# Hashed attention and a soft mixture of experts on one core: how the first two pairs of heads are prepared

## Chip, cores and metric

One NeuronCore of a Trainium2 chip. The metric is the device time of one execution in microseconds; three timed executions were taken of the kernel before, and one more with the hardware profiler on.

## What is computed

Two stages. Attention over 32 heads (4 batches of 8), 768 positions, 64 dimensions, in which a query may look only at keys whose six hash bits equal its own; its output, laid out as 3072 tokens of 512 values, goes through a soft mixture of 8 experts.

```python
q_bits = (einsum('bhsd,dk->bhsk', q, proj) > 0)      # k_bits likewise; six bits make a bucket
mask   = q_bucket[..., :, None] == k_bucket[..., None, :]
scores = where(mask, (q @ k.T) / sqrt(64), -1e9)
attn   = softmax(scores) @ v                           # per head, 768 x 768
x      = attn as [3072, 512]
logits = x @ phi                                       # 32 slots
slot   = softmax over tokens(logits).T @ x             # then per expert relu(. @ w1) @ w2
out    = softmax over slots(logits) @ slot_out
```

## The kernel before

Heads are handled in pairs; the two heads of a pair lie on partitions 0 to 63 and 64 to 127 of one transfer. All work is emitted from one sorted list (`plan`): `STEADY` gives the due time of each step relative to its head (the unit is a sixth of a head), `ONCE` gives it for single steps, mostly those of the opening and the end. Each engine runs what it was given in that order, so the table is an order written by hand for PE (TensorE), ACT (ScalarE), DVE (VectorE), POOL (GpSimd) and the DMA queues of SP, ACT and POOL.

For each head there is an operand tile `XY` (three of them rotate), with two halves `Y` and `X`, each of 128 partitions by 2 sides (x=0 queries, x=1 keys) by 768. In `Y`, rows 0 to 63 hold the high part of the values, row 64 a row of shifts (queries) or ones (keys), rows 65 to 76 the hash bits as penalties, rows 96 to 127 low parts; `X` holds the rest of the split. Rows 64 to 95 are zeroed once, and row 64 of the key side set to one, by `first_y` and `first_rows` (L281 to L290).

Per head: `smax` (L407) multiplies rows 0 to 95 and DVE takes the maximum of each row over nine PSUM tiles (L421, L424); `shift` (L434) makes of the maxima a 128 by 12 table in `mz`; `shift_rows` (L446) turns it on PE (L449), ACT copies it to `mr` (L452), and a DMA puts it into row 64 of `XY`. Only then may `scores` (L456) of that head run: two matmuls into one PSUM tile (L465), then the exponential on ACT (L469). POOL adds the exponentials up (`acc`, L471) into one of three sum tiles `acc0` to `acc2`, and `av` (L484) multiplies them with the values on PE (L494). In the steady part PE interleaves the scores of one head with the maxima of the next.

Before a pair's heads can start: `load` (L203) fetches raw queries and keys of the pair into `raw`, two planes of the tile `stage`; `bits` (L360) multiplies them with the projections (L357) and compares (`over`, L351); `split_hi` (L308, ACT, line L311) rounds to the high part; `split_lo` (L313, POOL line L321 for the first two pairs) leaves the low part; `spread_y`, `spread_l`, `spread_x`, `spread_bits` (L328 to L403) move the pieces by DMA to the rows of `XY` (line L325).

The opening, for head 0, goes by special steps: `first_bits` (L374) multiplies, and ACT copies the 64 rows of head 0 straight into `Y`; `first_over` compares on DVE straight into `Y`; `first_last` copies the products of the bits to a spare tile, from which POOL makes the bits of both heads (`bits_rest`, L393), which the DMAs spread to head 1. `copy_ident` rounds the identity on POOL, `first_mz` zeroes `mz`. `keep_warm` (L254) and `spin` (L428) are matmuls whose results nobody reads; a spin follows each maximum of head 0. The second pair's raw values go into the same `raw` planes as the first's.

Of the kernel before, what the change touches and what calls it, by code (L numbers as in the profile page):

```python
# [90 lines left out]
    ('load_weights', 16): 147.216379, ('load_weights', 17): 153.5946, ('load_weights', 18): 156.8062,
    ('load_weights', 19): 165.5946, ('load_weights', 2): 39.9087, ('load_weights', 20): 168.8062,
    ('load_weights', 21): 177.5946, ('load_weights', 22): 189.5946, ('load_weights', 3): 51.9087,
    ('load_weights', 4): 63.9087, ('load_weights', 5): 83.361725, ('load_weights', 6): 87.216379,
    ('load_weights', 7): 95.361725, ('load_weights', 8): 99.216379, ('load_weights', 9): 107.361725,
# [7 lines left out]
    ('scores', 8, 0, 1): 49.396684, ('scores', 9, 2, 0): 55.21665, ('shift_rows', 0): -3.614750908,  # L103
# [46 lines left out]
def lsh_attention_soft_moe(  # L150
# [130 lines left out]
    def first_y(i):  # L281
        for ts in (Ys, Xs):
            nc.gpsimd.memset(ts[i][64:96].bitcast(F32), 0.0)
# [789 lines left out]
```

## Time and profile before

| what | us |
|---|---|
| median of three timed runs | 481.88 (481.84 to 482.64) |
| the profiled execution's own time | 480.13 |
| its span, from first to last instruction | 478.4 |
| PE busy | 461.8 |
| POOL busy, DVE busy, ACT busy | 330.5, 364.4, 250.3 |
| mean granted TensorE clock | 0.989 of full |

Times of rows count from the span's start. A timeline row gives start, length, engine, line, operation, the tiles it writes and reads, how many instructions it merges, and in brackets the idle time of the engine before it with what ended it. PE rows overlap, since matmuls are pipelined, so the distance of starts says more than the length.

### The profile page before, as it was taken

The numbers are of one execution on the slowest core, as the hardware profiler recorded it, in microseconds if no ns is written. First come the engines' busy times: TensorE is split into PE (matmuls) and PEld (weight loads), VectorE is DVE, ScalarE is ACT, GpSimd is POOL, SyncE is SP. The second block draws the span as 40 slices with busy tenths as digits, with TensorE's granted clock in tenths as the row PEclk, the third lists the DMA queues.
The fourth block names the chain that finished last, engine by engine and source line by source line (L and its number), as shares of the span: only waits on it lengthen the run. The fifth ranks groups of instructions, "written<-read, shape, count | busy, mean of one in ns | idle before, by whom it ended". The sixth has DMA issues, their size and how long they took to land.

```text
span 478.4 us, 10738 instructions
## 1 busy us (share of the span) xinstructions
PE 461.8 (97%) x4012; PEld 290.6 (61%) x4012; DVE 364.4 (76%) x690; ACT 250.3 (52%) x465; POOL 330.5 (69%) x236
## 2 busy tenths in 40 slices
PE   7799999999999999999999999999999999989992
PEld 4466666666666666666666565656656666453581
DVE  5658897979798888888888888888989766463242
ACT  4365555564666464555655564646655455431242
POOL 7868776969595969696868696968859696602200
PEclk9799999999999999999999999999999999999998
DMA  5668587868575757777767676767758388979967
GB/s 149 186 164 198 145 180 218 181 170 185 172 174 160 161 136 160 224 173 209 189 168 196 173 216 167 213 166 224 195 169 223 112 214 317 393 295 388 408 267 299
DMA packets 39697, 99.71 MB, mean 208 GB/s; under 512 B 7422, under 2 KB 13708, under 8 KB 39644
## 3 DMA queue, kind: packets, MB, share of 16 engines
q1 hardware_dynamic: 39260, 98.16, 71.6%
q0 software_dynamic: 224, 0.47, 0.5%
q8 instruction: 32, 0.52, 0.5%
q10 hardware_dynamic: 160, 0.39, 0.3%
q14 instruction: 21, 0.17, 0.1%
HBM read 52.76 MB, written 6.29 MB: 123 GB/s over the span
## 4 chain that ended last, share of the span: by engine, by line
PE 90%; DMA 2%; POOL 2%; DVE 2%; issue 1%; ACT 1%; SPq 1%; DVEq 0%; ACTq 0%; POOLq 0%
PE st L465 29%; PE av L494 27%; PE smx L418 15%; PE qh L904 3%; PE mi L556 3%; PE mi L506 2%; PE mi L521 2%; PE qs L986 2%; PE mi L357 2%; DMA out<-w 1%; PE mi L541 1%; PE mi L711 1%; PE qa L949 1%; POOL stage L321 1%; PE mi L449 1%
## 5 line engine op out<-in xcount | busy, mean ns | idle before, releaser
L482 POOL TENSOR_TENSOR acc<-acc,pt 128x768 f32<-128x768 f32 x125 | 229.2, 1834 | 9.1
L469 ACT ACTIVATE pt<-st 128x512 f32<-128x512 f32 x288 | 164.1, 596 | 49.0 <-PE st L465 41.0
L465 PE MATMUL st<-XY 128*128 128x512 f32 (+1 forms) x768 | 180.1, 346 | 0.0
L424 DVE TENSOR_REDUCE mx<-smx 128x1 f32<-128x512 f32 x192 | 130.6, 688 | 28.8 <-PE smx L418 25.3
L465 PEld LDWEIGHTS st<-XY 128*128 128x128 f32 x768 | 129.5, 190 | 16.3 <-issue 0.6
L494 PE MATMUL av<-pt,v 128*32 128x384 f32 x1536 | 136.2, 488 | 0.0
L418 PE MATMUL smx<-XY 96*128 96x256 f32 (+1 forms) x384 | 117.8, 360 | 1.6 <-DMA XY<-bt 0.7
L476 POOL TENSOR_TENSOR acc<-pt 128x768 f32<-128x768 f32 x32 | 58.7, 1835 | 65.8 <-ACT pt L469 65.8
L494 PEld LDWEIGHTS av<-pt,v 128*32 128x32 f32 x1536 | 46.4, 110 | 70.7 <-issue 70.5
L418 PEld LDWEIGHTS smx<-XY 96*128 96x128 f32 x384 | 68.7, 191 | 29.6 <-DVE mx L424 8.8
L421 DVE TENSOR_REDUCE mx<-smx 128x2 f32<-128x512 f32 x96 | 64.8, 675 | 4.3 <-PE smx L418 3.8
L498 ACT COPY avs<-av 128x384 f32<-128x384 f32 x32 | 15.3, 478 | 89.9 <-PE av L494 89.9
L318 DVE TENSOR_REDUCE stage<-stage 128x768 fp32r<-128x1536 f32 x28 | 50.1, 1790 | 0.0
L513 DVE RECIPROCAL sm<-sm 128x128 f32<-128x128 f32 x45 | 38.1, 896 | 0.0
L558 DVE TENSOR_TENSOR xq<-mi,r 128x256 f32<-128x256 f32 x45 | 17.6, 418 | 26.2 <-PE mi L556 26.2
L311 ACT ACTIVATE stage<-stage 128x768 fp32r<-128x768 f32 x30 | 24.9, 840 | 9.0 <-DMA stage<-qk 6.7
L556 PEld LDWEIGHTS mi<-ident,avs 128*128 128x128 f32 x90 | 10.2, 141 | 10.6 <-issue 10.0
L509 ACT ACTIVATE sm<-mi,eps 128x384 f32<-128x384 f32 x15 | 8.7, 582 | 13.8 <-PE mi L506 13.8
L943 POOL CAST avs<-lacc 128x48 fp32r<-128x48 f32 x8 | 2.1, 266 | 19.6 <-ACT lacc L934 12.5
L556 PE MATMUL mi<-ident,avs 128*128 128x128 f32 x90 | 15.7, 282 | 0.0
L986 PE MATMUL qs<-w 128*32 128x128 f32 (+1 forms) x360 | 15.5, 305 | 0.0
L904 PE MATMUL qh<-w,siT 128*32 128x512 f32 x128 | 14.6, 595 | 0.0
(179 smaller groups left out, 334.6 us busy)
## 6 DMA issues: line engine op xcount, KB each, us to landing
w<-w SPq DMA_DIRECT2D x61, 512.0 KB
XY<-stage SPq DMA_DIRECT2D x62, 384.0 KB
stage<-qk SPq DMA_DIRECT2D x32, 384.0 KB
XY<-stage SPq DMA_DIRECT2D x62, 192.0 KB
v<-vt SPq DMA_DIRECT2D x32, 192.0 KB
out<-w SPq DMA_DIRECT2D x12, 512.0 KB
xq<-w SPq DMA_DIRECT2D x3, 512.0 KB
XY<-bt SPq DMA_DIRECT2D x62, 19.5 KB
```

The source lines that it names most:

```text
L318: nc.vector.tensor_reduce(out=w[:, 2 * x + 1], in_=stage[:, x:n + 1:n - x].rearrange("p t s -> p s t"), axis=AX.X, op=ALU.add, negate=True)
L418: nc.tensor.matmul(pt[:, o:o + b - a], Ys[h % N_Y][0:96, 0, t * P:(t + 1) * P], Ys[h % N_Y][0:96, 1, a:b], start=True, stop=True)
L421: nc.vector.tensor_reduce(out=mx[:, n - 1:n + 1], in_=pt.rearrange("p (a x) -> p a x", a=2), axis=AX.X, op=ALU.max)
L424: nc.vector.reduce_max(out=mx[:, n:n + 1], in_=pt, axis=AX.X)
L465: nc.tensor.matmul(pt[:, o:o + b - a], x[:, 1, i * P:(i + 1) * P], x[:, 0, a:b], start=first, stop=not first)
L469: nc.scalar.activation(pts[i // 2][:, 512 * u:512 * u + 512], pt, AF.Exp, scale=D ** -0.5)
L476: nc.gpsimd.tensor_tensor(out=s["acc"], in0=pr[:, 0:S], in1=pr[:, S:2 * S], op=ALU.add)
L482: eng.tensor_tensor(out=s["acc"], in0=s["acc"], in1=pr[:, a * S:(a + 1) * S], op=ALU.add)
L494: nc.tensor.matmul(s["av"][D * c + d:D * c + d + 32, 0:HC], s["v"][:, i, d:d + 32], pr[:, o + c * HC:o + (c + 1) * HC], start=(i == 0), st ...
L513: nc.vector.reciprocal(out=rs[:, k * P:(k + 1) * P], in_=rs[:, k * P:(k + 1) * P])
L556: nc.tensor.transpose(pt[:, o:o + P], st[h + a]["avs"][:, k * P:(k + 1) * P], ident)
L904: nc.tensor.matmul(ph[fh][32 * j:32 * j + 32], siT[:, k, 4 * g + j, :], wt[0, g, k, j][:, fh * 512:(fh + 1) * 512], start=(k == 0), stop=( ...
```

## The change

The opening is laid out anew; nothing changes in `STEADY`. Raw values of the first pair come in halves of 64 partitions (head 0's keys, head 0's queries, then head 1's), behind the small transfer `first`; the remaining constants (`cst`) come later. The second pair's raw values go to the sum tiles `acc1` and `acc2`, which nobody uses yet, and are issued right behind. Zero rows and rows of ones are written by memsets in place, two of them on DVE, and no DMA carries them any more. `first_bits` multiplies only head 0's 64 rows, with 512 and 256 columns; a new step `more_bits` multiplies all 128 rows into one PSUM tile, which ACT copies for `bits_rest`. The comparisons for head 0 are five (one of 512, four of 256 columns). Twelve spins stand in the table at places of their own, reading the keys' side, and `keep_warm` is called for two matmuls at the start instead of seven, with the later lot of three gone.

```diff
-    def load(h, xs=(0, 1)):
-        for x in xs:
-            nc.sync.dma_start(out=raw[:, x], in_=qk[x, h // 2])
+    def raws(h, x):
+        return accs[1 + x] if h == 2 else raw[:, x]
+
+    def load(h):
+        for x in range(2):
+            nc.sync.dma_start(out=raws(h, x), in_=qk[x, h // 2])
+
+    def load_half(a):
+        for x in (1, 0):
+            nc.sync.dma_start(out=raw[D * a:D * a + D, x], in_=qk[x, 0, D * a:D * a + D])
...
-    load(0, (1,))
     nc.sync.dma_start(out=pre[:, 0:C_ID + 64], in_=first[:, 0:C_ID + 64])
-    load(0, (0,))
-    nc.sync.dma_start(out=pre[:, C_ID + 64:], in_=cst[:, C_ID:C_FD])
+    load_half(0)
+    load_half(1)
...
-    keep_warm(7, True)
+    keep_warm(2, True)
...
-    row = accs[0][0:1]
-    nc.gpsimd.memset(row, 1.0)
+    nc.vector.memset(Ys[0][64:96].bitcast(F32), 0.0)
+    nc.vector.memset(XYs[2][64:96, 0].bitcast(F32), 0.0)
...
-    def first_y(i):
-        for ts in (Ys, Xs):
-            nc.gpsimd.memset(ts[i][64:96].bitcast(F32), 0.0)
-
     def first_rows(i):
-        for ts in (Ys, Xs)[i == 0:]:
-            if i == 1:
-                move(ts[i][64:96], Xs[0][64:96], nc.gpsimd)
-            else:
-                nc.gpsimd.dma_start(out=ts[i][ROW:ROW + 1, 1].bitcast(F32), in_=row)
+        ts = XYs[i] if i else Xs[0]
+        nc.gpsimd.memset((ts[64:96, 1] if i == 2 else ts[64:96]).bitcast(F32), 0.0)
+        nc.gpsimd.memset(ts[ROW:ROW + 1, 1].bitcast(F32), 1.0)
...
+    def first_copy(x):
+        nc.scalar.copy(Ys[0][0:64, x], raw[0:64, x])
+
+    def first_bits(x):
+        first_pt[x] = p_st.tile([P, 512], F32, name="st")
+        for c, (a, b) in enumerate(((0, 512), (512, S))):
+            j = 2 * x + c
+            nc.tensor.matmul(first_pt[x][32 * j:32 * j + 32, 0:b - a], pb[0:D, 32 * x:32 * x + 32], raw[0:D, x, a:b],
+                             start=True, stop=True)
+
+    def first_hi(x):
         w = parts_of(0)
+        nc.scalar.copy(w[:, 2 * x], raw[:, x])
+
+    def more_bits():
+        pt = p_mi.tile([P, 512], F32, name="mi")
+        for x in range(2):
+            bits_of(0, x, pt)
...
+        nc.scalar.copy(pts[0][:, 0:HC], pt[:, 0:HC])
...
-        if h == 0 and n % 4 != 1:
-            spin(1)
```

ACT, from its first cast on: in the kernel before (L380, L382, L386 in `first_bits`, L390 and L391 in `first_last`, L349 `first_x`, L311 `split_hi` of the second pair, L452 the row of shifts, L325 the DMAs `spread_x` and `spread_l` of head 0).

```order
L380 CAST XY_134<-stage 64x768
L382 CAST stage<-stage 128x768
L380 CAST XY_134<-stage 64x768
L386 CAST stage<-stage 128x768
L390 COPY pt_82<-st 64x384
L391 COPY pt_82<-st 64x384
L349 COPY XY_134<-stage 64x768
L325 DMA XY_134<-stage 32x2x768
L349 COPY XY_134<-stage 64x768
L311 ACTIVATE stage<-stage 128x768 x2
L452 CAST mr<-mi 12x128
L325 DMA XY_134<-stage 32x2x768
```

And in the changed kernel (L391 `first_copy`, L402 `first_hi`, L409 the copy in `more_bits`, L327 `split_hi`, L365 `first_x`, L468 the row of shifts).

```order
L391 CAST XY_130<-stage 64x768
L402 CAST stage<-stage 128x768 x2
L409 COPY pt_82<-mi 128x384
L391 CAST XY_130<-stage 64x768
L327 ACTIVATE stage<-acc_86 128x768
L327 ACTIVATE stage<-acc_87 128x768
L341 DMA XY_130<-stage 32x2x768
L365 COPY XY_130<-stage 64x768
L341 DMA XY_130<-stage 32x2x768
L468 CAST mr<-mi 12x128
L365 COPY XY_130<-stage 64x768
```

The two `split_hi` of the second pair have moved from just ahead of the row of shifts to ahead of head 0's DMAs, and read the sum tiles; the copy of head 0's queries (the second L391) has moved behind the copy of the bits' products.

PE, from head 0's last maximum to its first scores, before (L418 `smax`, L432 `spin`, L449 the turn of `mz`, L357 the second pair's bits; `XY_134` is head 0, `XY_135` head 1).

```order
L418 MATMUL smx<-XY_134 128x256 x2
L432 MATMUL av<-XY_134 128x512
L449 MATMUL mi<-ident,mz 128x128
L357 MATMUL mi<-stage,pb 32x384 x4
L418 MATMUL smx<-XY_135 128x512 x2
L418 MATMUL smx<-XY_135 128x256 x2
L418 MATMUL smx<-XY_135 128x512 x2
L465 MATMUL st<-XY_134 128x512 x4
```

And in the changed kernel (L436 `smax`, L448 `spin`, L373 the bits, L465 the turn, L481 scores; `XY_130` is head 0, `XY_131` head 1).

```order
L436 MATMUL smx<-XY_130 128x512 x2
L448 MATMUL av<-XY_130 128x512 x2
L373 MATMUL mi<-acc_86,pb 32x384 x2
L373 MATMUL mi<-acc_87,pb 32x384 x2
L448 MATMUL av<-XY_130 128x512
L465 MATMUL mi<-ident,mz 128x128
L436 MATMUL smx<-XY_131 128x512
L436 MATMUL smx<-XY_131 128x256 x2
L448 MATMUL av<-XY_130 128x512
L436 MATMUL smx<-XY_131 128x512
L448 MATMUL av<-XY_130 128x512
L436 MATMUL smx<-XY_131 128x512 x2
L481 MATMUL st<-XY_130 128x512 x2
```

The bits of the second pair have moved from behind the turn to ahead of it, with three spins; ahead of the first scores stand five tiles of head 1's maxima in both (a pair of 256 columns is one tile), with two spins among them now.

POOL, from the first memset to the second pair's low parts, before (L283 `first_y`, L290 and L325 the DMAs of `first_rows`, L279 `ident`, L321 `split_lo`, L352 `bits_rest`).

```order
L276 MEMSET acc_85 1x768
L283 MEMSET XY_134 32x2x768 x2
L290 DMA XY_134<-acc_85 1x16x48
L325 DMA XY_135<-XY_134 32x2x768 x2
L279 CAST ident<-pt_83 128x128
L321 ISA
L321 TENSOR_TENSOR stage<-stage 128x768 x2
L273 MEMSET mz 128x128
L352 TENSOR_SCALAR bt<-pt_82,con 128x384
L283 MEMSET XY_136 32x2x768 x2
L290 DMA XY_136<-acc_85 1x16x48 x2
L321 TENSOR_TENSOR stage<-stage 128x768 x2
```

And in the changed kernel (L305 and L306 `first_rows`, L368 `bits_rest`, L337 `split_lo`, L295 `mz`, L301 `ident`).

```order
L305 MEMSET XY_131 32x3072
L306 MEMSET XY_131 1x1536
L368 ISA
L368 TENSOR_SCALAR bt<-pt_82,con 128x384
L337 TENSOR_TENSOR stage<-stage 128x768
L305 MEMSET XY_130 32x2x768
L306 MEMSET XY_130 1x768
L295 MEMSET mz 128x128
L301 CAST ident<-pt_83 128x128
L337 TENSOR_TENSOR stage<-stage 128x768
L305 MEMSET XY_132 32x1536
L306 MEMSET XY_132 1x1536
```

The DMAs are gone, `bits_rest` has moved from behind both low parts of the first pair to ahead of them, and head 0's zero rows stand between the two low parts; those of the second pair follow these rows in both.

## Rows read from the trace of the kernel before

**Rows 1.** The page: PE's busy time with its share of the span, and the granted TensorE clock in 40 slices of the span, in tenths of full.

```profile
PE 461.8 (97%) x4012; PEld 290.6 (61%) x4012; DVE 364.4 (76%) x690; ACT 250.3 (52%) x465; POOL 330.5 (69%) x236
...
PEclk9799999999999999999999999999999999999998
```

**Rows 2.** Windows of the opening and of the long middle: stretch in us, its length, busy us of each engine (instructions), granted clock, DMA share, GB/s.

```profile
0.00:4.00 4.00, 2.90 (x14) 2.30 (x14) 0.80 (x6) 1.73 (x3) 3.43 (x7) 1.00 0.51 150
4.00:10.82 6.82, 4.40 (x24) 2.29 (x23) 4.49 (x9) 3.83 (x6) 4.23 (x7) 1.00 0.56 142
10.82:14.23 3.41, 3.41 (x11) 2.49 (x9) 2.86 (x5) 1.58 (x2) 3.41 (x3) 0.50 0.91 233
14.23:21.06 6.83, 4.15 (x20) 1.85 (x18) 4.40 (x10) 1.83 (x3) 6.71 (x6) 1.00 0.58 162
21.06:24.47 3.41, 3.36 (x8) 2.34 (x8) 1.81 (x3) 0.98 (x2) 0.60 (x1) 0.50 0.67 160
...
40.00:475.03 435.03, 428.00 (x3829) 268.30 (x3821) 339.20 (x641) 229.14 (x430) 299.84 (x209) 1.00 0.74 213
```

**Rows 3.** The chain of work that ended last, its part in the opening: start us, us, what.

```profile
4.50 2.55 DMA XY<-acc
...
8.85 3.59 POOL stage L321 x2
...
12.58 1.66 POOL bt L352
...
16.84 1.93 DMA XY<-bt
...
26.16 0.23 PE smx L418
```

**Rows 4.** SP's DMA issues in the opening.

```profile
0.74 0.40 SPq L205 DMA_DIRECT2D stage<-qk  x1
1.20 0.42 SPq L223 DMA_DIRECT2D pt<-first  x1
...
10.68 2.11 SPq L205 DMA_DIRECT2D stage<-qk  x2
...
18.43 0.77 SPq L325 DMA_DIRECT2D XY<-mr  x1
```

**Rows 5.** ACT in the opening.

```profile
6.21 0.83 ACT L380 CAST XY<-stage 64x768 fp32r<-64x768 f32 x1 [0.89 <-DMA stage<-qk]
...
7.80 0.47 ACT L390 COPY pt<-st 64x384 f32<-64x384 f32 x1
...
17.42 0.84 ACT L311 ACTIVATE stage<-stage 128x768 fp32r<-128x768 f32 x1 [1.74 <-DMA stage<-qk]
...
18.17 0.24 ACT L452 CAST mr<-mi 12x128 fp32r<-12x128 f32 x1
```

**Rows 6.** DVE in the opening.

```profile
1.12 0.48 DVE L227 MEMSET phs<- 128x512 f32 x1
3.94 0.23 DVE L235 TENSOR_TENSOR pb<-pt 128x64 f32<-128x64 f32 x1 [2.33 <-DMA pt<-first]
...
5.18 1.38 DVE L352 TENSOR_SCALAR XY<-st,con 16x384 fp32r<-16x384 f32 x2 [0.94 <-PE st L357]
...
8.44 0.69 DVE L424 TENSOR_REDUCE mx<-smx 128x1 f32<-128x512 f32 x1 [0.65 <-PE smx L418]
...
13.12 0.69 DVE L424 TENSOR_REDUCE mx<-smx 128x1 f32<-128x512 f32 x1 [0.17 <-PE smx L418]
13.98 1.35 DVE L424 TENSOR_REDUCE mx<-smx 128x1 f32<-128x512 f32 x2 [0.16 <-PE smx L418]
15.26 0.69 DVE L421 TENSOR_REDUCE mx<-smx 128x2 f32<-128x512 f32 x1
...
16.48 0.17 DVE L442 SCALAR_TENSOR_TENSOR mz<-mi,mz 128x6 f32<-128x6 f32 x1
```

**Rows 7.** PE in the opening.

```profile
6.23 0.84 PE L357 MATMUL st<-stage,pb 128*32 128x384 f32 x4 [1.17 <-DMA stage<-qk]
...
7.93 0.47 PE L418 MATMUL smx<-XY 96*128 96x512 f32 x1 [0.22 <-DVE XY L352]
...
15.06 0.42 PE L432 MATMUL av<-XY 96*128 96x512 f32 x1
16.79 0.30 PE L449 MATMUL mi<-ident,mz 128*128 128x128 f32 x1 [1.31 <-DVE mz L442]
17.02 1.26 PE L357 MATMUL mi<-stage,pb 128*32 128x384 f32 x8
...
22.14 1.91 PE L465 MATMUL st<-XY 128*128 128x512 f32 x4
...
29.33 4.08 PE L494 MATMUL av<-pt,v 128*32 128x384 f32 x48
```

**Rows 8.** POOL in the opening.

```profile
0.74 0.73 POOL L276 MEMSET acc<- 1x768 f32 x1 [0.29 <-POOLq L1064]
1.50 2.69 POOL L283 MEMSET XY<- 32x1536 f32 x2
...
8.51 0.29 POOL L279 CAST ident<-pt 128x128 fp32r<-128x128 f32 x1
...
27.34 1.83 POOL L476 TENSOR_TENSOR acc<-pt 128x768 f32<-128x768 f32 x1 [5.68 <-ACT pt L469]
```

More of the change, by code (lines that the diff above doesn't have):

```diff
@@ L91 @@
[L91 to L95, printed above, removed]
+    ('batch_top_exp',): 195.7222, ('batch_turn', 3): 195.723, ('bits', 2): -23.689255146,
@@ L115 @@
+    ('spread_y', 27): 150.008401, ('spread_y', 29): 162.008401, ('spread_y', 3): 6.008401,
+    ('spread_y', 31): 174.008401,
 }
@@ L320, in split_lo @@
         else:
-            nc.gpsimd.tensor_tensor(out=w[:, 2 * x + 1], in0=raw[:, x], in1=w[:, 2 * x], op=ALU.subtract)
+            nc.gpsimd.tensor_tensor(out=w[:, 2 * x + 1], in0=raws(h, x), in1=w[:, 2 * x], op=ALU.subtract)
     def move(dst, src, eng=nc.sync):
@@ L349, in first_x, with over @@
         nc.scalar.copy(Xs[0][0:64, x], st[0]["w4"][0:64, 3 * x])
-    def over(out, pt, rows, eng=nc.vector):
-        eng.tensor_scalar(out=out, in0=pt[rows, 0:HC], scalar1=con[rows, C_TH:C_TH + 1],
+    def over(out, pt, rows, eng=nc.vector, cols=slice(0, HC)):
+        eng.tensor_scalar(out=out, in0=pt[rows, cols], scalar1=con[rows, C_TH:C_TH + 1],
                           scalar2=con[rows, C_AM:C_AM + 1], op0=ALU.is_gt, op1=ALU.mult)
@@ L357, in bits_of @@
             nc.tensor.matmul(pt[32 * j:32 * j + 32, 0:HC], pb[:, 32 * x:32 * x + 32],
-                             raw[:, x, (j % 2) * HC:(j % 2 + 1) * HC], start=True, stop=True)
+                             raws(h, x)[:, (j % 2) * HC:(j % 2 + 1) * HC], start=True, stop=True)
     def bits(h):
@@ L368, in lsh_attention_soft_moe, with first_over @@
     first_pt = {}
[L370 to L391 removed]
+    def first_over(x, a, b):
+        j = 2 * x + a // 512
+        over(Ys[0][64:80, x, a:b], first_pt[x], slice(32 * j, 32 * j + 16), cols=slice(a % 512, a % 512 + b - a))
+    def first_copy(x):
[7 more added lines that the diff above has]
+    def first_hi(x):
+        w = parts_of(0)
+        nc.scalar.copy(w[:, 2 * x], raw[:, x])
[3 more added lines that the diff above has]
+            bits_of(0, x, pt)
+        st[0]["bt"] = st[1]["bt"] = pp.tile([P, HC], F32R, name="bt", bufs=1)
+        nc.scalar.copy(pts[0][:, 0:HC], pt[:, 0:HC])
     def bits_rest():
@@ L776, in at @@
         plan.append((when, len(plan), (f, *args)))
-    first_y(0)
-    first_rows(0)
-    for i in range(1, N_Y):
-        if i > 1:
-            at(first_y, i)
+    for i in range(N_Y):
         at(first_rows, i)
@@ L785, in lsh_attention_soft_moe @@
     at(load_phi)
-    at(keep_warm, 3, True, tag="a")
+    at(load_cst)
     at(copy_ident)
-    at(first_bits)
-    at(first_last)
+    for n in (1, 0):
+        at(first_copy, n)
+        at(first_bits, n)
+        at(first_hi, n)
+    for xab in ((1, 0, 512), (0, 0, 256), (1, 512, S), (0, 256, 512), (0, 512, S)):
+        at(first_over, *xab)
+    at(more_bits)
+    for n in range(12):
+        at(spin, 1, tag=n)
     at(bits_rest)
```

82 lines of the change are left out of this document (40 added, 42 removed).

## The prediction

> **What bounds the kernel now.** First the page [rows 1]: TensorE (PE) is busy 461.8 us, 97% of the span; the only slices in which its granted clock is below full are in the first 25 us and at the end. Then the windows [rows 2]: from 40 to 475 us PE is busy 428.0 of 435.0 us at clock 1.00, so there time is PE work, and nothing in this change alters that work. A change of the opening can help only by letting PE reach its unbroken stretch sooner. In the PE rows [rows 7] that stretch starts with the first scores (L465) at 22.14 us; I take as the finishing line the first attend block (L494) at 29.33 us, because the change leaves PE's list behind it as it was. A shift of this block should reach the end nearly whole: what follows (weights, output) is issued as PE frees buffers, so it moves with it.
>
> What made PE wait until 22.14 us? The chain [rows 3] goes back through GpSimd (POOL): the zero rows and the row of ones for the first head, whose DMA takes 2.55 us; the two low parts, 3.59 us; the bits of the pair, 1.66 us; the DMA of those bits, 1.93 us; then the second head's maxima. Beside it runs a second chain that ends within a step of it: first head's maxima on VectorE (DVE), from 8.44 to 15.95 us [rows 6]; the shift (three small operations, to 16.64 us); its turn on PE at 16.79 us [rows 7]; and the copy of the result on ScalarE (ACT), which begins only at 18.17 us [rows 5], since ACT stands until 17.42 us for the second pair's raw values and then works 0.84 us on them. Those were issued only from 10.68 us on, as they go into the buffer that the first pair leaves [rows 4]. The row of shifts is sent at 18.43 us [rows 4].
>
> The clock is the third thing [rows 2]: 1.2 GHz (0.50) in 10.82 to 14.23 us, behind a stretch in which PE was busy 4.40 of 6.82 us, and again in 21.06 to 24.47 us, behind one with 4.15 of 6.83 us. The second low stretch lies on the first scores.
>
> **The change, part by part.** *Second pair at once, into the sums' buffers.* ACT's copy of the shift row no longer stands behind raw values: they are issued at about 3.1 and 3.5 us. The first sum buffer used so is written late (the first sum of all, in another buffer, is at 27.34 us [rows 8]), so the buffers are free. Gain: up to 18.17 - 17.09 = 1.1 us on the second chain. Issue of each transfer stays at 0.4 us [rows 4].
>
> *Zero rows in place.* POOL loses the 0.73 us memset, two memsets of 1.35 us each from its early list, the wait for its own DMA and two DMA issues, 8.51 us in all before `ident` [rows 8]. It gains one memset of 2.7 us and one of 1.4 us (two times 0.73), ended near 4.9 us, before the values for the bits exist. The bits then start when ACT has copied them (8.0 us below) and are done at 9.7, against 14.24; one low part follows to 11.5, and the rest of the list (2.1 us of memsets, `mz`, `ident`) ends about 14.0, before the shift at 16 us and the turn. So the first chain becomes some 4 us shorter and drops out. DVE takes over two memsets of 1536 elements: 512 took 0.48 us [rows 6], so 1.3 to 1.45 us each, on DVE from about 3.3 us to 6.1 us, in front of the first comparisons. Five of these (one of 512, four of 256 columns; two of 384 took 1.38 us [rows 6]) end at about 8.7 us. They are covered by the step below, with 0.5 us to spare.
>
> *Halves.* In before, the bits of x=0 started at 6.23 us when their 384 KB landed [rows 7]. The new queue has the same bytes ahead of the last half (without one 64 KB piece), in four transfers for two. I take 6.2 us for the last half; it can't well land before 5.3 (the last issue at 2.6 us, and 2.7 from the issue of the small `first` to its use [rows 4, 6]). No row shows raw values fetched by halves. The Trainium skill (DMA: Bandwidth & Descriptors, Rules for kernel authors) speaks against this edit: two transfers to disjoint halves of the partitions share the same engines and serialize, so one transfer is as good. By that rule the last half lands as the whole did, at 6.2 us, and the sum stays as below; with a last half at 5.3 us it would be 0.9 us less. An earlier first half is worth nothing here for a reason in the order: the first maxima need `first_copy` of x=0, and this now stands last on ACT, behind the bits of both halves.
>
> So: last half 6.2, eight bit matmuls 1.26 [rows 7] to 7.5, their copy 0.47 [rows 5] to 8.0, `first_copy` 0.83 [rows 5] to 8.8, matmul to maximum 0.51 (7.93 to 8.44 us [rows 6, 7]): **first maximum at 9.3 us**, 0.9 us later than before. But then nine follow without a gap: 0.65 us apart at full clock (13.98, two in 1.35 [rows 6]), I take 0.68: the seventh ends at 14.1, the ninth at 15.4, the shift is ready at 16.1.
>
> *The turn.* PE's list has, between the ninth maximum's matmul and the turn, two spins, the bits of the second pair and one more spin. At 0.06 + 0.24 for the matmul, 0.45 a spin (15.06 us row, 0.42 [rows 7]) and 1.26 for the bits this is 14.1 + 0.3 + 0.9 + 1.26 + 0.45 = **17.0 us**, later than the shift: the bits were behind the turn in before and are ahead of it now, price up to 0.9 us. Turn 0.30, cast 0.24 [rows 5, 7]: sent at 17.65 us, against 18.43.
>
> *The row's trip.* Bounds: 1.93 us from issue to landing of the last bits, and 3.71 us from the row's issue (18.43) to the first scores (22.14), in which other work also lay [rows 3, 4, 7]. I take 2.7, near the 2.55 of the other single-row DMA [rows 3]. First scores 20.35 us. The second head's maxima don't delay that: both orders put five of its nine tiles ahead of the first scores; from 17.2 us at 0.65 the third ends near 19.5 and the fifth matmul near 20.0. The edit named last in the change is thus worth nothing by itself.
>
> *Clock.* PE drops five of its first seven fp32 matmuls and all three of the second lot, and gets twelve spins for nine. Ahead of 4 us PE had worked 2.90 us [rows 2]; now about 0.9 us there and the bits from 3.6 on. So I allow for 1.2 GHz on the first bits (1.26 us become 2.5 if all run so, of which 0.5 is met if the last half lands at 5.7) and for one low stretch somewhere before the scores. At 0.86 us a tile for 0.65 (from 13.12 to 13.98 us, [rows 6]), four tiles cost 0.8; over the bits it costs 1.3; in front of the maxima next to nothing: I add 0.5. First scores: **20.9 us**, 1.2 us sooner.
>
> *From there to the attend block.* 12 matmuls of 512 columns and 12 of 256 for the scores, 4 and 6 for maxima, at 0.235 and 0.12 (0.23 for one of 512 [rows 3]), and a turn of 0.11: 3.76 + 2.16 + 0.11 = 6.0 us at full clock. Before took 29.33 - 22.14 = 7.2, of which 2.3 us fell in the low stretch. With a full clock, as PE is busier ahead of 21 us: 1.2 us more. Attend block at 26.9: **2.4 us gained**. The profiled execution took 480.13 us (span 478.4), so 477.7 for it; the median of the three timed runs is 481.88, 1.75 us above it, and the same step from there gives **479.5 us**.
>
> **Rivals.** (1) *The clock falls on the first scores again.* PE still waits for the row until 20.9 us, and in before such a stretch brought 0.50. The Trainium skill (TensorE: Matmul & The Clock Gate, HAM oscillation) has the same warning: gaps throttle the array again; both low stretches of this trace agree with it. Against it: spins now lie between the second head's maxima. Price 1.2 to 1.7 us: 480.9.
> (2) *Only the wait changes its name.* Last half late, first maximum at 10, a low clock on maxima and bits: first scores at 22, clock as before: no change, 481.9.
> (3) *Slower.* The bits in front of the turn are the place: at 1.2 GHz spins and bits take 2.6 us more, the turn comes at 19.6 and the first scores at 23.0; with the low stretch on the scores too (7.7 us to the attend block, as all 3.4 us of it then count) the block is at 30.7, 1.4 us late: 483.3. It decides at a turn later than 18.3 us. For it: the list has eight warming matmuls fewer at the start.
> (4) *More:* half landed at 5.3, no low stretch after 8 us, row's trip 2.0: scores at 19.0, attend block at 25.0: 477.6.
>
> **How the numbers follow.** About 0.2% (1 us) is what a measurement can tell from no change. Forecast 0.50 (own range 478.7 to 480.4), rival 1 0.20 (480.2 to 481.5), rival 2 0.12, rival 3 0.09, rival 4 0.09. Faster than 480.9: forecast, rival 4 and half of rival 1, 0.70; within: the other half and nearly all of rival 2, 0.21; slower 0.09. The range leaves out rival 3 and the far half of 4 and of 2: 478.0 to 481.8.
>
> **What would show it.** Right: first maximum near 9.3 us and nine without gaps; the turn near 17, its cast at once; first scores near 21 at clock 1.00; the attend block at 26 to 27.5; the same spacing of all that follows. Wrong: the turn waiting on PE's bits past 18 us; a low stretch on the scores; POOL's low part or memsets named as releaser of the shift or of the second head's rows; or the lead lost between 30 us and the end.

## Result and profile after

The changed kernel takes 484.09 us (median of 7 runs, 482.71 to 486.25) against 481.84 us (480.64 to 482.64) for the kernel before on the same chip: ratio 1.0053, 95% interval 1.0035 to 1.0071, 2.3 us slower. Forecast was 2.4 us faster. The profiled execution took 482.71 us. Its page, to be held against [rows 1]:

```profile
span 480.9 us, 10726 instructions
...
PE 466.0 (97%) x4007; PEld 289.8 (60%) x4007; DVE 367.6 (76%) x693; ACT 249.8 (52%) x464; POOL 330.8 (69%) x232
...
PEclk9999999999999999999999999999999999999998
```

PE is busy 4.2 us longer, with five instructions fewer: nearly the same matmuls, at a lower clock and, as the rows below show, with spins that wait for each other. The clock row hides it, and so does the clock column of the windows (length, then busy us of PE, PEld, DVE, ACT, POOL with counts, granted clock, DMA share, GB/s):

```profile
7.00:14.35 7.35, 6.90 (x20) 3.21 (x20) 4.92 (x9) 3.83 (x7) 4.47 (x3) 1.00 0.55 162
14.35:23.45 9.10, 8.79 (x25) 4.44 (x25) 5.46 (x12) 1.51 (x3) 8.79 (x9) 1.00 0.49 112
23.45:31.20 7.75, 7.56 (x41) 5.97 (x40) 6.90 (x14) 4.87 (x10) 2.83 (x3) 1.00 0.59 165
...
42.00:477.00 435.00, 428.34 (x3829) 268.31 (x3821) 338.98 (x640) 228.86 (x430) 299.97 (x209) 1.00 0.74 213
```

1.00 is printed wherever no record of the clock precedes, and the first record of this execution is a rise at 23.45 us. (So it is in the first window of [rows 2] too: the first record there is the rise at 4.0 us.) What PE had before that is read from its rows: start, length, line, operation, count, idle time before.

```profile
7.59 1.50 PE L373 MATMUL mi<-stage,pb 128*32 128x384 f32 x8 [0.34 <-DMA stage<-qk]
9.02 1.65 PE L448 MATMUL av<-XY 96*128 96x512 f32 x2
10.47 1.17 PE L436 MATMUL smx<-XY 96*128 96x512 f32 x3
11.44 1.48 PE L448 MATMUL av<-XY 96*128 96x512 f32 x2
12.72 1.05 PE L436 MATMUL smx<-XY 96*128 96x512 f32 x2
13.57 0.63 PE L448 MATMUL av<-XY 96*128 96x512 f32 x1
...
18.44 1.48 PE L448 MATMUL av<-XY 96*128 96x512 f32 x2
19.85 1.51 PE L373 MATMUL mi<-acc,pb 128*32 128x384 f32 x8
21.29 0.80 PE L448 MATMUL av<-XY 96*128 96x512 f32 x1
21.88 0.42 PE L465 MATMUL mi<-ident,mz 128*128 128x128 f32 x1
...
25.12 0.63 PE L481 MATMUL st<-XY 128*128 128x512 f32 x2
25.59 0.40 PE L436 MATMUL smx<-XY 96*128 96x256 f32 x2
...
31.20 3.11 PE L510 MATMUL av<-pt,v 128*32 128x384 f32 x36
```

From 12.72 us two maxima take 0.85 us, up to the start of the spin at 13.57: 0.43 for each 512 columns. From 25.12 us two matmuls of 512 columns take 0.47. So PE ran at 1.2 GHz over bits, all first maxima and the turn, and at 2.4 GHz from 23.45 us: no low stretch lies on the scores, unlike [rows 2]. In a pair of spins the second starts 0.69 to 0.85 us behind the first (9.02 and 9.88, 11.44 and 12.12 us): each spin takes the one buffer of its pool anew and waits until the spin before it has ended, so PE also waits within its own list. The rest of the chain to the turn and beyond, rows of DVE, ACT, POOL and SP against [rows 4 to 6] and [rows 8]:

```profile
11.25 0.69 DVE L442 TENSOR_REDUCE mx<-smx 128x1 f32<-128x512 f32 x1 [1.52 <-PE smx L436]
...
18.25 1.29 DVE L442 TENSOR_REDUCE mx<-smx 128x1 f32<-128x512 f32 x2 [1.01 <-PE smx L436]
...
20.06 0.17 DVE L458 SCALAR_TENSOR_TENSOR mz<-mi,mz 128x6 f32<-128x6 f32 x1
...
22.33 0.26 ACT L468 CAST mr<-mi 12x128 fp32r<-12x128 f32 x1 [7.46 <-PE mi L465]
...
15.71 0.29 POOL L301 CAST ident<-pt 128x128 fp32r<-128x128 f32 x1
...
22.65 0.83 SPq L341 DMA_DIRECT2D XY<-mr  x1
```

The shift is ready at 20.23 us, the turn comes at 21.88, behind spins and bits; ACT, which had been waiting 7.46 us, copies at once; POOL's part of the turn was done by 16.0 us. Against before the attend block is 1.86 us late, the third head's outputs 3.5 and all later heads 2.9, the end 2.6 (480.94 and 478.35 us). The extra us comes at 47 us, in the chain of waits:

```profile
40.15 1.43 SPq L341
41.62 6.30 DMA XY<-stage
47.92 0.14 issue
48.06 0.94 PE st L481 x3
```

The third head's `spread_x` stands in SP's list behind the fourth head's pieces and lands when PE wants to begin its scores.

### The profile page after: what moved, and what is told of

The parts are those of the page before. It is cut to its first block, busy times and chain, and to the rows that moved or that the text cites. A ratio compares the mean times of both kernels' runs of the same rounds, so it can differ in the third digit from the quotient of the medians.

```text
span 480.9 us, 10726 instructions
## 1 busy us (share of the span) xinstructions
PE 466.0 (97%) x4007; PEld 289.8 (60%) x4007; DVE 367.6 (76%) x693; ACT 249.8 (52%) x464; POOL 330.8 (69%) x232
## 4 chain that ended last, share of the span: by engine, by line
PE 89%; DMA 4%; SPq 2%; DVE 2%; ACT 1%; issue 1%; POOL 0%; DVEq 0%; ACTq 0%
PE st L481 27%; PE av L510 25%; PE smx L436 15%; PE qh L923 3%; PE mi L572 3%; PE mi L522 2%; PE mi L373 2%; PE mi L537 2%; PE qs L1005 2%; SPq L341 2%; DMA out<-w 1%; PE av L448 1%; DMA XY<-stage 1%; PE mi L557 1%; DMA stage<-qk 1%; PE mi L727 1%
## 5 line engine op out<-in xcount | busy, mean ns | idle before, releaser
L481 PE MATMUL st<-XY 128*128 128x512 f32 (+1 forms) x768 | 179.8, 345 | 0.6 <-DMA XY<-stage 0.3
L481 PEld LDWEIGHTS st<-XY 128*128 128x128 f32 x768 | 129.0, 190 | 17.2 <-issue 0.6
L436 PE MATMUL smx<-XY 96*128 96x256 f32 (+1 forms) x384 | 118.7, 364 | 0.4 <-DVE mx L439 0.2
L436 PEld LDWEIGHTS smx<-XY 96*128 96x128 f32 x384 | 69.4, 194 | 28.6 <-DVE mx L442 9.2
L327 ACT ACTIVATE stage<-stage 128x768 fp32r<-128x768 f32 x28 | 23.1, 840 | 9.5 <-DMA stage<-qk 6.3
L572 PEld LDWEIGHTS mi<-ident,avs 128*128 128x128 f32 x90 | 10.2, 141 | 10.6 <-issue 10.0
```

The source lines that it names most:

```text
L436: nc.tensor.matmul(pt[:, o:o + b - a], Ys[h % N_Y][0:96, 0, t * P:(t + 1) * P], Ys[h % N_Y][0:96, 1, a:b], start=True, stop=True)
L481: nc.tensor.matmul(pt[:, o:o + b - a], x[:, 1, i * P:(i + 1) * P], x[:, 0, a:b], start=first, stop=not first)
L572: nc.tensor.transpose(pt[:, o:o + P], st[h + a]["avs"][:, k * P:(k + 1) * P], ident)
```

## Experiments

Medians against the kernel before beside each (ratio with its 95% interval); "low" is what the profile shows of 1.2 GHz ahead of the attend block. "From the start", or "to" a time, means that the first record is the rise at that time; in the other rows the first record is a rise at 3.9 to 6.6 us, and what lies ahead of it is left out. Marks are of the profiled execution, us; its own time is in the last column, and where it lies 1.3 us or more off the median (before, after, e3, e5, e7, f13, f16) the marks need not be those of the median execution.

| run | median | ratio | low | turn | first scores | block | own |
|---|---|---|---|---|---|---|---|
| before | 481.84 | 1 | 10.82–14.23, 21.06–24.47 | 16.79 | 22.14 | 29.33 | 480.13 |
| after | 484.09 | 1.0053 (1.0035–1.0071) | from the start to 23.45 | 21.88 | 25.12 | 31.20 | 482.71 |
| e1 | 483.67 | 1.0027 (1.0007–1.0048) | to 27.37 | 21.64 | 25.45 | 32.55 | 484.38 |
| e2 | 483.89 | 1.0046 (1.0029–1.0063) | to 23.71 | 22.10 | 25.35 | 31.43 | 483.73 |
| e3 | 484.58 | 1.0057 (1.0036–1.0077) | to 23.34 | 20.31 | 25.30 | 31.36 | 482.54 |
| e4 | 485.89 | 1.0087 (1.0066–1.0108) | to 27.55 | 21.49 | 25.29 | 32.38 | 485.96 |
| e5 | 483.72 | 1.0037 (1.0016–1.0058) | 11.75–21.99 | 20.59 | 23.83 | 29.88 | 480.96 |
| e7 | 484.34 | 1.0045 (1.0028–1.0063) | 13.39–27.05 | 20.0 | 25.53 | 32.34 | 485.75 |
| e6 | 483.22 | 1.0027 (1.0009–1.0044) | to 16.83, 23.66–27.07 | 18.79 | 22.98 | 30.66 | 483.15 |
| e8 | 484.24 | 1.0055 (1.0036–1.0074) | 11.81–25.47 | 16.79 | 25.38 | 31.57 | 483.92 |
| e9 | 480.51 | 0.9962 (0.9948–0.9976) | to 14.35, 21.18–24.59 | 18.40 | 21.80 | 29.12 | 480.51 |
| e10 | 482.89 | 1.0008 (0.9988–1.0029) | 8.67–15.49, 18.91–25.73 | 18.12 | 23.05 | 30.35 | 482.44 |
| e11 | 484.04 | 1.0060 (1.0034–1.0086) | 16.26–29.91 | 16.30 | 24.58 | 33.13 | 484.17 |
| e12 | 481.40 | 0.9987 (0.9973–1.0001) | 9.87–16.70, 23.53–26.94 | 18.54 | 22.65 | 30.33 | 481.57 |
| f13 | 483.92 | 1.0036 (1.0022–1.0050) | to 16.80, 20.22–27.04 | 19.11 | 23.81 | 31.36 | 482.49 |
| f14 | 480.55 | 0.9972 (0.9961–0.9982) | 7.46–14.29, 21.12–24.53 | 18.42 | 21.79 | 29.11 | 481.01 |
| f15 | 480.86 | 0.9987 (0.9974–0.9999) | to 16.48 | 19.39 | 22.50 | 28.57 | 480.14 |
| f16 | 482.60 | 1.0017 (0.9998–1.0036) | 10.75–27.82 | 16.68 | 22.69 | 31.16 | 486.43 |
| f17 | 480.78 | 0.9994 (0.9977–1.0010) | to 15.18, 22.00–25.42 | 18.70 | 21.81 | 29.65 | 480.80 |
| f18 | 481.48 | 0.9993 (0.9975–1.0010) | to 22.00 | 20.02 | 23.52 | 30.04 | 482.10 |

### One part undone in the changed kernel

**e1**, warming:
```diff
-    keep_warm(2, True)
+    keep_warm(7, True)
```


> Changed kernel with seven warming matmuls at the start again instead of two. Theory 'clock': the changed kernel runs PE at 1.2 GHz from the start to 23.45 us, because two matmuls do not lift it; with seven it is lifted near 4 us, first scores come before 22.5 us (25.1 now), the attend block before 28.5 (31.2), the time is 481.0 or less (484.1 now). Rival 'raw values': the late last half (7.6 us) and ACT's order hold the chain; attend block at 30.5 or later, time 483.4 or more.

Three of its twelve times are 480.96 to 481.39, the other nine 483.26 to 485.27. The profiled one, of the nine, kept 1.2 GHz to 27.37 us, and its mean granted clock is 0.995, since the stretch without a record counts as full; the three have 0.986, as e5's profile below has with its early rise. So warming lifts the clock early in some executions; in the median it is not the main cause.

**e2**, two whole transfers:
```diff
-    load_half(0)
-    load_half(1)
+    for x in (1, 0):
+        nc.sync.dma_start(out=raw[:, x], in_=qk[x, 0])
```


> Changed kernel with the first pair's raw values in two whole transfers (keys first) instead of four halves. Theory 'halves': a transfer to 64 partitions runs at about half the rate, so whole ones land the last raw value near 6.2 us instead of 7.6, and the first maximum comes about 1.3 us sooner; time 482.8 to 483.3. Theory 'clock' alone: PE stays at 1.2 GHz and paces the maxima, less than 0.5 us comes out at the end, 483.6 or more.

No difference. The first maximum came at 11.47 us, 0.2 later than with halves: the whole pair was there sooner, but PE at 1.2 GHz worked on its bits without a wait to 7.81 us.

**e3**, the second pair's bits behind the turn:
```diff
-    ... ('bits', 2): -23.689255146,
+    ... ('bits', 2): -20.02,
```


> Changed kernel with the second pair's bits behind the turn of the first head's shifts, as in the kernel before. Theory 'bits ahead of the turn': the turn comes when the shift is ready, 20.3 us instead of 21.9, and the first scores 1 to 1.6 us sooner, 482.5 to 483.1. Rival: the second head's maxima, which then wait for the comparison of these bits on DVE, hold the first scores just as long; within 0.4 us of the changed kernel, 483.7 to 484.4.

The turn is 1.57 us earlier and the first scores are where they were: the bits then stand ahead of the second head's maxima, for which the scores wait as well. So the edit that I had named for rival 3 was not it. The wait at 47 us was gone, and the time no better.

**e4**, the third head's `spread_x` earlier:
```diff
-    ... ('spread_x', 2): 9.510813397,
+    ... ('spread_x', 2): 6.0,
```


> Changed kernel with the queries' side of head 2 (spread_x of head 2) issued on SP ahead of head 3's pieces instead of behind them. Theory 'queue': head 2's scores wait 1 us for these pieces in the changed kernel; issued early they don't, the heads from the third on are 1.9 us late against the kernel before instead of 2.9, time 483.0 to 483.3. Rival: contention of the transfers, whatever their order; 483.8 or more.

Worse: the piece now stands ahead of the fourth head's bits on SP, and PE waits 1.6 us for those (DMA `XY<-bt`) instead.

**e5**, `keep_warm(15, True)`, and **e7**, the same with e2's and e3's edits:

> Changed kernel with fifteen warming matmuls at the start, without a gap until the first bits. Theory 'clock': the run with seven fell into two groups of times (three of twelve near 481.1, the others 483.3 to 485.3), so seven lift the clock only sometimes; fifteen lift it before 8 us in nearly every execution. The first bits then start near 7 us instead of 4.5 but at 2.4 GHz, the first maximum comes by 11.5, the turn by 19, the attend block by 28.5; median 480.5 to 481.5. Rival: the raw values and ACT's order set the opening; two groups or one near 484 stay, median 483 or more.

> Changed kernel with fifteen warming matmuls, whole transfers of the first pair's raw values, and the second pair's bits behind the turn. If the parts add up: turn by 17.5 us, first scores by 21, attend block by 27, median 479.5 to 480.5, below the kernel before. If the maxima of the second head behind the bits set the first scores: as with fifteen warming matmuls alone, 480.5 to 481.5.

In both a rise near 5 to 6.6 us is lost again at 11.75 and 13.39 us, over the first maxima, and does not come back before 21.99 and 27.05 us. Warming at the start sets where the clock begins, and does not keep it there; e5's profile is the fastest of its twelve executions, 2.8 us under their median.

### The kernel before, with one part changed

**e6**, `keep_warm(2, True)` and none of the later three:

> Kernel before with two warming matmuls at the start instead of seven, and without the later three: only this part of the change. Theory 'clock': PE stays at 1.2 GHz through the first head's maxima or longer, median 1 to 2.5 us above the kernel before. Rival: POOL's chain and not PE set the first scores in the kernel before, so the clock up to 20 us costs it nothing; within 0.5 us of the kernel before.

1.3 us slower. Cold as the changed kernel is, it rises at 16.83 us, among the first maxima. Its list there differs from the changed one in the spins, among other things.

**e8**, a spin behind each of the second head's five tiles too:
```diff
-        if h == 0 and n % 4 != 1:
+        if h == 0 and n % 4 != 1 or h == 1 and n in (0, 2, 3, 8, 11):
```


> Kernel before with one more spin behind each of the five second-head maxima that stand ahead of the first scores. Theory 'clock': PE has fewer gaps from 19 to 22 us, the low stretch on the first scores (21.06 to 24.47 us) falls away more often, median 0.5 to 1.2 us below the kernel before. Rival: gaps at 18.3 to 19.0 us remain and the clock falls as before; within 0.4 us.

Slower, for a reason of its own: spins of this kernel read the queries' side, whose row of shifts is on its way.

```profile
21.41 0.77 PE L432 MATMUL av<-XY 96*128 96x512 f32 x1 [1.61 <-DMA XY<-mr]
```

**e11**, the second pair into the sums' buffers at once, alone:
```diff
-    ... ('load', 2): -12.762070462,
+    ... ('load', 2): -60.0,
...
+    def raws(h, x):
+        return accs[1 + x] if h == 2 else raw[:, x]
```


> The kernel before with one part of the change alone: the second pair's raw values go to the sums' buffers at once. Theory: the copy on ScalarE no longer stands behind them, the row of shifts is sent 0.7 to 1.1 us earlier (17.4 to 17.8 us for 18.43), but GpSimd's chain (zero rows, low parts, bits, their DMA) ends where it did and holds the second head's maxima, so first scores move by less than 0.6 us and the median lies within 0.5 us of the kernel before. Rival, the row alone decides: scores and block 1 us earlier, median 481.0.

Neither theory: 2.2 us slower. POOL's and SP's rows:

```profile
4.50 0.66 POOL L293 DMA_DIRECT2D XY<-acc  x1 [0.31 <-POOL XY L286]
9.15 1.12 POOL L328 DMA_DIRECT2D XY<-XY  x2 [3.99 <-DMA XY<-acc]
...
14.42 1.65 POOL L355 TENSOR_SCALAR bt<-pt,con 128x384 fp32r<-128x384 f32 x1
...
16.09 3.29 SPq L328 DMA_DIRECT2D XY<-bt  x4
19.43 0.72 SPq L328 DMA_DIRECT2D XY<-stage  x1
20.26 0.77 SPq L328 DMA_DIRECT2D XY<-mr  x1
```

With 768 KB more in flight POOL's one-row DMA took 4.4 us for 2.6 [rows 3], everything behind it on POOL came 1.84 us later, and the row of shifts, copied at 17.33 us, stood on SP behind four issues of bits to 20.26. So in this kernel the edit costs time as long as the rows go through POOL's queue.

**e12**, those rows written in place by POOL and the bits ahead of the second low part, on top of e11:
```diff
+        if i == 1:
+            nc.gpsimd.memset(XYs[1][64:96].bitcast(F32), 0.0)
+        ts = XYs[i] if i else Xs[0]
+        nc.gpsimd.memset(ts[ROW:ROW + 1, 1].bitcast(F32), 1.0)
...
-    ... ('bits_rest',): -37.319143276, ...
+    ... ('bits_rest',): -50.0, ...
-    ... ('first_last',): -38.392596163, ...
+    ... ('first_last',): -50.5, ...
```


> The kernel before with two parts of the change: the sums' buffers as above, and the zero rows and rows of ones written in place by GpSimd memsets with no DMA; the bits of both heads on GpSimd ahead of the second low part. Whole transfers, seven warming matmuls and the spins behind each maximum stay. Theory, both chains were needed: row sent near 17.5 us, first scores near 20.3 for 22.1, block near 27.5 to 28 for 29.3, median 480 to 481, faster than both kernels. Rival, the clock falls on the scores whenever they come after a wait: scores earlier, but the block within 0.7 us of before, median 481.5 to 482.3.

2.6 us faster than e11, level with before. The row was sent no earlier (19.15 us): a copy of 128 by 3 values on DVE, 0.16 us long in the kernel before, took 2.56 us, and the first comparisons began at 7.00 us for 5.18 [rows 6]. DVE's rows, and POOL's beside them:

```profile
4.29 2.56 DVE L240 COPY con<-pt 128x3 f32<-128x3 f32 x1
7.00 2.78 DVE L352 TENSOR_SCALAR XY<-st,con 16x384 fp32r<-16x384 f32 x4 [0.15 <-PE st L357]
...
4.17 2.65 POOL L288 MEMSET XY<- 32x3072 f32 x1
```

The copy ends at 6.85 us, with POOL's memset (6.82). In the changed kernel the same copy took 0.72 us, from 2.70 to 3.42, and the same memset there ended at 3.39.

**f16**, no spins behind the first maxima:
```diff
-        if h == 0 and n % 4 != 1:
-            spin(1)
```


> The kernel before without the nine spins behind the first head's maxima (matmuls that nobody reads), nothing else. Theory, the spins without a gap bring the clock back: after its fall at about 10.8 us it does not rise before the second head's maxima or the scores, turn at 17.5 us or later, block at 31 us or later (29.3), median 483.5 to 485. Rival, the spins are idle ballast: the same or 0.3 us faster.

In the theory's direction, and smaller: +0.7 us, with an interval that takes in 1, and times from 481.04 to 486.43. The profiled execution, the longest, shows what the theory said, 0.50 over all 17 us. What the shorter ones had is not shown: their mean granted clock, 0.976 to 0.989 for 0.978 here, does not set them apart.

```profile
10.75:27.82 17.07, 14.85 (x39) 8.45 (x40) 10.44 (x19) 5.79 (x9) 10.74 (x9) 0.50 0.67 184
```

### The spins put back in the changed kernel

**e9**, a spin behind each of the first head's nine tiles, as before, and none in the table:
```diff
             nc.vector.reduce_max(out=mx[:, n:n + 1], in_=pt, axis=AX.X)
+        if h == 0 and n % 4 != 1:
+            spin(1)
...
-    for n in range(12):
-        at(spin, 1, tag=n)
```


> The changed kernel with its twelve spins taken from their places in the table and put back behind each of head 0's nine maxima, as the kernel before has them; nothing else differs (two warming matmuls, halves, bits ahead of the turn). Theory, the spins' places: at 1.2 GHz a tile of maxima with its spin keeps PE without a gap, so the clock comes up within the first maxima (about 15 to 17 us in place of 23.4), the turn at 20 us or before (21.9), first scores at 23 or before (25.1), attend block by 29.5 (31.2); median 482.0 to 482.8. Rival, the start of the clock alone (fewer warming matmuls): the clock stays at 1.2 GHz until the second head's maxima as in the changed kernel, turn past 21, block past 31, median 483.5 or more.

By the medians 3.6 us faster than the changed kernel (4.4 by the two ratios), 1.3 faster than the kernel before. PE's rows, and the windows up to and on the scores:

```profile
10.06 0.80 PE L436 MATMUL smx<-XY 96*128 96x512 f32 x1 [1.33 <-ACT XY L391]
10.66 0.63 PE L450 MATMUL av<-XY 96*128 96x512 f32 x1
11.08 0.63 PE L436 MATMUL smx<-XY 96*128 96x256 f32 x2
...
13.22 0.63 PE L450 MATMUL av<-XY 96*128 96x512 f32 x1
13.64 0.63 PE L436 MATMUL smx<-XY 96*128 96x256 f32 x2
14.07 0.53 PE L450 MATMUL av<-XY 96*128 96x512 f32 x1
14.44 0.40 PE L436 MATMUL smx<-XY 96*128 96x256 f32 x2
...
17.00 0.85 PE L373 MATMUL mi<-acc,pb 128*32 128x384 f32 x8
18.40 0.30 PE L467 MATMUL mi<-ident,mz 128*128 128x128 f32 x1 [0.54 <-DVE mz L460]
```

```profile
14.35:21.18 6.83, 5.47 (x24) 2.63 (x23) 6.41 (x13) 1.20 (x3) 6.52 (x8) 1.00 0.69 153
21.18:24.59 3.41, 3.39 (x9) 2.81 (x10) 1.95 (x3) 1.02 (x2) 2.81 (x2) 0.50 0.70 240
```

From 11.08 us maxima and spins start 0.43 us apart, and the wait of a spin for the one before it is covered by the maxima between them; at 14.35 us the clock rises, and the bits take 0.85 us for 1.51. The turn waits 0.54 us for the shift, not for PE's list. The edit does two things at once: spins no longer stand in pairs among the maxima, and one spin instead of three stands between the last maximum and the turn.

**e10**, e9 with e1's and e3's edits; **f13**, e9 with e3's; **f14**, e9 with e1's; **f15**, e9 with e2's:

> The same, with seven warming matmuls at the start for two and the second pair's bits on PE behind the turn. Theory: the clock is lost at most for one stretch, as in the kernel before; turn at 18 to 19 us (shift ready decides, no bits ahead), first scores at 21 to 22, block at 28 to 29; median 481 to 482, no slower than the kernel before. Rival (halves and the second pair's transfers make the first bits so late that nothing is left, or the bits only move the clock's loss to the scores): block past 30, median 483 or more.

> The version with spins back (480.51 us), with one more edit: the second pair's bits on PE behind the turn. If the bits behind the turn are what lost the 2.4 us of the combined version (PE is idle ahead of the turn and the clock falls in front of the scores): median 482 to 483.5, a second low stretch after 16 us. If only the order counts: turn 17.9 for 18.4, first scores within 0.5 us, median 480.0 to 480.8.

> The version with spins back (480.51 us), with one more edit: seven warming matmuls at the start for two. If the warming sets the phase of the clock so that it falls again on the bits and then on the scores: a rise near 5 us, a fall near 9 to 12 us, median 481.5 to 483. If warming only helps: the first bits at 2.4 GHz, first maximum 0.6 us earlier (10.2 to 10.4), median 479.5 to 480.5.

> The version with spins back (480.51 us), with the first pair's raw values in two whole transfers for four halves. Theory, the halves cost time: four half issues and their slower packets made the last values land at 7.2 to 7.5 us against 6.2; with whole transfers the bits of both sides end sooner, the first maximum comes 0.5 to 1 us earlier (9.9 to 10.4), median 479.6 to 480.2. Rival (the order on ScalarE, with the copy of the first head's values last, or the queue, holds the first maximum where it is): within 0.3 us of 480.5.

f13 settles e10: the bits behind the turn cost 3.4 us here (with seven warming matmuls, e10 against f14, 2.3). PE stands idle 1.37 us ahead of the turn, and 1.2 GHz lies on 20.22 to 27.04 us, second maxima and scores, with bits and maxima between turn and scores:

```profile
16.80:20.22 3.42, 2.05 (x14) 0.83 (x13) 1.83 (x6) 0.77 (x2) 3.30 (x3) 1.00 0.63 141
20.22:27.04 6.82, 6.27 (x15) 4.39 (x16) 5.01 (x8) 1.41 (x3) 3.80 (x3) 0.50 0.51 150
```

This execution is the fastest of the six (482.49 us), so it accounts for 2.0 of the 3.4 us; the others have a lower mean granted clock still, 0.983 to 0.986 for 0.990.

f14: warming adds nothing (first maximum 10.92 us; the theory that it helps had 10.2 to 10.4): a rise at 4.05 us is lost at 7.46 and comes back at 14.29. f15: whole transfers add nothing either; the first maximum comes later, at 11.46 us.

**f17** and **f18**, e9 with one and with two spins behind each of the second head's first two tiles:
```diff
+        if h == 1 and n in (0, 2):
+            spin(1)
```


> The version with spins back (480.51 us), and one spin more behind each of the first two tiles of the second head's maxima, where its TensorE waited 0.55 us for VectorE. If these waits bring the low stretch on the scores (21.18 to 24.59 us): it is gone or shorter, the attend block at 28.0 to 28.6 us for 29.1, median 479.5 to 480.1. If the wait for the shift ahead of the turn brings it, or the spins themselves come in the way: median 480.3 to 481.5.

> The same with two spins each in place of one. If the waits decide: as with one or better, median 479.4 to 480.1. If the spins now stand in the way of the maxima (two are 0.47 us at full clock in a wait of 0.55, and 0.86 us at 1.2 GHz): first scores later by 0.3 to 0.6 us, median 480.5 to 481.5.

Neither is better than e9: in f17 the low stretch stays on the scores (22.00 to 25.42 us). f18's profile has none there, but also 0.43 us between starts from 11.19 to 18.02 us without a rise, which came only at 22.00 us: rows without a wait do not bring the clock back at a fixed time. Its two spins of one call share a tile and start 0.43 us apart (21.14 and 21.57 us), so the wait in the changed kernel's pairs is that of the buffer, not of the matmul. Pairs in one tile at the changed kernel's places were not tried.

f18's profile also tells the list from the clock, since it has 1.2 GHz up to 22.00 us, nearly as long as the changed kernel:

```profile
10.60 0.80 PE L436 MATMUL smx<-XY 96*128 96x512 f32 x1 [1.32 <-ACT XY L391]
...
18.02 0.63 PE L452 MATMUL av<-XY 96*128 96x512 f32 x1
18.58 1.51 PE L373 MATMUL mi<-acc,pb 128*32 128x384 f32 x8
20.02 0.48 PE L469 MATMUL mi<-ident,mz 128*128 128x128 f32 x1
...
21.14 1.02 PE L452 MATMUL av<-XY 96*128 96x512 f32 x2
```

At the same clock its nine maxima are 0.85 us apart, for 0.95 in the changed kernel, and from the ninth to the turn it is 1.76 us for 3.02, with one spin there for three. The turn comes 1.9 us sooner than in the changed kernel without any help of the clock. So about half of e9's 3.5 us at the turn is the spins' own time on PE; the rest came with the rise at 14.35 us and an earlier first maximum.

## Why the prediction was wrong

**The step that failed is "Clock"**: 0.5 us for 1.2 GHz on the first bits and one low stretch, "in front of the maxima next to nothing". PE had 1.2 GHz until 23.45 us, so that the sum's prices at full clock, 0.68 us a tile, 0.45 a spin and 1.26 for the bits, held nowhere ahead of the turn. By the sum's own stations, prediction and profiles:

| station | predicted | after | e9 | f18 |
|---|---|---|---|---|
| bits on the last half begin | 6.2 | 7.59 | 7.23 | 7.77 |
| first maximum | 9.3 | 11.25 | 10.89 | 11.43 |
| ninth maximum begins | 14.7 | 18.86 | 16.88 | 18.26 |
| turn | 17.0 | 21.88 | 18.40 | 20.02 |
| first scores | 20.9 | 25.12 | 21.80 | 23.52 |
| attend block | 26.9 | 31.20 | 29.12 | 30.04 |

Of the 4.9 us at the turn, 1.95 had arisen at the first maximum (1.4 of it with the last half), 2.2 over the nine maxima (0.95 us a tile for 0.68) and 0.7 over spins and bits. I had counted the spins, twelve for nine, and taken them as cover against the clock; where each stands I used only for their 0.45 us. Two by two, the ratios show what the places of the spins and of the bits are worth:

| | bits ahead of the turn | bits behind |
|---|---|---|
| spins in the table | 1.0053 (after) | 1.0057 (e3) |
| spins behind each maximum | 0.9962 (e9) | 1.0036 (f13) |

Neither placement gains without the other: with the bits behind the turn the spins' places change nothing clear of noise, and with the spins in the table the bits' place changes nothing. With the bits ahead, as the change has them, the spins' places are shown as the cause of the loss, worth 3.6 us by the medians. Their number is not it: f18 has thirteen, at 481.48 us. In the kernel before, taking the spins out costs less (f16). Through what the places act is shown in part: the waits within pairs and the spins ahead of the turn account for about half at the turn, at an unchanged clock (f18); that they also decide when the clock rises is not shown, since f18, with e9's list up to 20 us, rose at 22.00. **Rival 3** had the mechanism in part: 1.2 GHz on spins and bits, decided by a turn later than 18.3 us (it came at 21.88). Its reason, fewer warming matmuls, holds in the kernel before (e6, 1.3 us), here in three executions of twelve (e1), and not with the spins back (f14). The Trainium skill (TensorE: Matmul & The Clock Gate, HAM oscillation) warns of gaps that throttle the array again. Ahead of the two low stretches of before there are such gaps, of 1.17 and 1.31 us [rows 7]. The late rise of the changed kernel it does not explain: PE's idle times there from 7.59 to 23.45 us are 0.06 to 0.19 us each, and f18, with none from 11.19 us on, had 1.2 GHz to 22.00 all the same.

**"The bits were behind the turn and are ahead of it now, price up to 0.9 us"** looked at the turn alone. In the changed kernel moving them back brings the turn 1.57 us sooner and the scores no sooner (e3). With the spins back the price has the wrong sign: the bits fill PE's wait for the shift, and moved back they cost 3.4 us (f13), in the profile with 1.2 GHz on the second maxima and the scores.

**"Last half 6.2"** was 1.4 us early. Most of that was PE: it worked on head 0's bits from 4.50 to 7.25 us, at 1.2 GHz, and then waited 0.34 us for the transfer. The halves did not matter to the time: e2 and f15 take them away and gain nothing. The sentence that by the Trainium skill (DMA: Bandwidth & Descriptors, Rules for kernel authors) one transfer is as good is borne out by the medians (e9 and f15 within 0.35 us), not by the first maximum, which halves bring 0.2 to 0.6 us sooner.

**"What follows moves with it"** missed SP's order: 1.05 us at the third head, which no sentence of the sum looked at. Its removal in e3 and its move in e4 gained nothing, so its own worth stays open.

**Right:** POOL's chain dropped out (shift at 20.2, POOL done by 16.0); ACT copied the row at once; turn to first scores 3.24 us, predicted 3.35 ahead of the clock (where the row's sending at 17.65 us is 0.11 more than turn and cast add up to); first scores to the attend block 6.08, predicted 6.0, at full clock and so without rival 1; the middle has PE 428.34 us busy in 435 [rows 2]. With the spins back the first scores come 0.34 us sooner than before and the low stretch lies on them, which is rival 1's profile; its 480.9 stands beside e9's 480.51. (That the two are close is luck: e9 is another kernel.)

**Open:** why the rise comes at 14.35, 16.80 or 22.00 us in lists alike up to there (e9, f13, f18). And the profiles of before and e9 are level at the block (29.33, 29.12) and near level at the end, where the medians differ by 1.3. Part of that is settled by the times: the profiled execution of before, 480.13 us at a mean granted clock of 0.989, is not a common one. Of the 119 executions of the kernel before that were timed beside the experiments, 14 have 0.989 or more, with a median of 480.8 us; the other 105 have less, with a median of 482.0. So most executions have more of 1.2 GHz on record than the one from which the prediction set out [rows 2], and e9's gain over the median need not show against that profile.

## What to carry to other kernels

Filler matmuls are worth their places, not their number: put each where the engine would otherwise wait, between work that has its operands, never two in a row that take one buffer in turn, and none between the last maximum and the step that all wait for, unless the engine stands idle there. Real work that fits into such a wait (the bits ahead of the turn) is better still; look at what the engine does in the wait before calling a move a loss. Before a profile is taken as the starting point, see whether its execution is a common one. And hold the clock against the distance of starts before believing a clock column, since it says 1.00 before the first record.

## What was not expected of the hardware

- The same program's executions differ in the clock: e1 has three times near 481.1, all with a mean granted clock of 0.986, and nine of 483.3 and more at other values. The clock is not all of it: f16 spreads over 5.4 us, and its 482.08 and its 486.43 have 0.977 and 0.978.
- A small copy on DVE can be held by a memset on POOL: in all 15 runs in which it began 0.4 us or more before the memset's end it ended 0.02 to 0.03 us behind that end, and took 0.52 to 0.72 us, in e12 2.56; in the other five (before, e6, e8, e11, f16) it began at the memset's end or behind it, or at most 0.12 us before, and took 0.16. DVE's TENSOR_TENSOR just ahead of it took 0.23 us beside the same memset (after, e12) as in before.
- Transfers that nobody waits for delay small ones: 768 KB more in flight took POOL's 3 KB row from 2.6 to 4.4 us (e11).
- A warmed array can lose its clock on the first work itself: with fifteen warming matmuls it had 2.4 GHz from 4.92 us, was busy 5.98 of the next 6.83 us, and had 1.2 GHz from 11.75 to 21.99 us (e5).
